# One kernel for hashed attention and two dense layers: issue order read from a table, one weight step fewer, second key copy by DMA

## The chip, the cores and the metric

The kernel runs on one core of a Trainium2 chip. The metric is device time in microseconds (us), the median of a few executions. The core has five instruction streams: PE (TensorE, matmuls; its weight loads are shown as PEld), DVE (VectorE), ACT (ScalarE), POOL (GpSimd) and SP (SyncE, which here only issues DMAs). Each stream executes its instructions in the order in which the program lists them, and waits on semaphores for the other streams.

## The reference

```python
q_bits = (einsum('bhsd,dk->bhsk', q, proj) > 0);  k_bits = the same with k
mask   = bucket(q_bits)[..., None] == bucket(k_bits)[..., None, :]
scores = where(mask, q @ k.T / sqrt(D), -1e9)
attn   = exp(scores - max);  attn /= attn.sum + 1e-9
x = (attn @ v) with the heads side by side          # 1536 x 512
h = x @ w_in;  g = 0 (h <= -1), (h+1)**2/4, h (h >= 1)
x = g @ moe_w_out                                    # d_ff 2048
out = ((x @ w_a) * (x @ w_b)) @ moe2_w_out           # d_ff 1536
```

Two batches of 8 heads, 768 positions, head size 64. The weights of the dense layers arrive as 64-bit floats, seen as pairs of 32-bit words.

## The kernel before

**Recording and ordering.** The kernel does not call the engines directly. Every step is recorded with `add(engs, emit, r, w)` as an operation: which engines could do it and at what estimated cost, what it reads, what it writes. `Program.schedule` then runs an event-driven list scheduler over the recorded operations with these costs and with hand-tuned ranks and biases (`TUNE`), and so chooses an engine for every operation and one issue order; `issue` emits them in that order. An operation that several engines can do (a copy on ACT or DVE, a subtraction on DVE or POOL) is thus placed by the scheduler.

**Attention.** For each of 16 heads, keys are loaded (`load_head`, tile `kn`), doubled along the free dimension by a copy on ACT or DVE, transposed on PE (`tk`) and split into a high and a low part (`kh`, `kl`). Queries are split (`qs`), transposed (`tq`) and scaled (`qt`). `signs` forms all projections' signs in one PSUM bank (`kp`, constants `zq_h`, `zq_l`, `zk`), `buckets` turns them into rows that go next to the parts (`q` copy, `kid`, `kl`). `qk` makes six score tiles of 128x768 for a head: matmuls (`s`), a minimum on DVE (`mn`, L602), the exponential on ACT (`sm`, L604), then `phi`, the fp16 part of it (ACT or DVE), `plo`, the rest (POOL or DVE, L384), a DMA transpose of each pair of tiles (`pth`, `ptl`), and `pv` on PE. Each score tile so costs DVE at least one `mn`, ACT one `sm`, and four elementwise steps in all. There are 96 score tiles.

**Weights.** Each of 71 matrices of 512 KB is loaded as `stage` and turned from 64-bit into 32-bit floats in five steps in `conv_one`: absolute value of the upper word on ACT (L847), a maximum with 2^-15 ("clamp", L850, DVE or POOL), a shift with a mask (L852, DVE), and two steps that join sign and lower bits (L855, L858, DVE, each with two inputs from SBUF). The result `F` or `wab` is split into a high and a low part (`whi`/`wlo`, `wkh`/`wkl`).

**Dense layers.** Tokens are taken in four blocks of 384. `hp`, `ap` and `bp` are the first contractions of the two layers (L953, twelve matmuls each), `acc` the second ones (L1001, L1037). The first two blocks' dense work is interleaved with the attention of the second batch. DVE, ACT and POOL do the elementwise steps between (`t`, `gh`, `gl`, `xs`).

**Start.** Twelve matmuls on zeros warm up PE; the projections are fetched by two DMAs from POOL's queue and turned into `zq_h`, `zq_l`, `zk` by nine DVE instructions before the recorded operations begin.

Of the kernel before, what the change touches and what calls it, by code (L numbers as in the profile page):

```python
# [23 lines left out]
T0 = 130  # L24
LEAST = 2.0 ** -15


class Buf:
    """A tile that is allocated when the first operation that writes it is issued."""

    def __init__(self, tag, shape, dtype, name=None):
# [15 lines left out]

class Program:
    """Records operations with the buffers they touch, orders them for all engines by list
    scheduling with estimated costs, and issues them in that order."""  # L50

    PRICE = {"pe": 0.0, "act": 0.3, "dve": 1.7, "pool": 0.2, "sp": 0.0}
    PRICE2 = {"pe": 0.0, "act": -2.5, "dve": 2.5, "pool": 1.3, "sp": 0.0}
    FLAT = ("acc", "y", "xn")
    TUNE = {
# [1095 lines left out]
```

## Time and profile before

| what | value |
|---|---|
| median of 3 runs | 862.54 us (862.17 to 863.79) |
| span of the profiled execution, first to last instruction | 861.3 us |
| the profiled execution's own time | not listed; its span is 1.2 us below the median |
| PE busy | 801.6 us (93%) |
| DVE / ACT / POOL busy | 588.1 (68%) / 511.6 (59%) / 192.3 us (22%) |
| mean granted TensorE clock | 0.972 of full speed |

Busy time is the time in which an engine executes at least one instruction; successive instructions of one engine overlap a little, so their durations add up to more than its busy time. "Idle before" an instruction is put down to what released it last.

### The profile page before, as it was taken

To read this page: it belongs to the slowest core of one execution; us is meant where nothing else is said; L and a number is where in the kernel's file an instruction comes from. 1 tells how busy PE (TensorE), PEld (TensorE's weight loads), DVE (VectorE), ACT (ScalarE), POOL (GpSimd) and SP (SyncE) were. 2 spreads that over 40 slices of the span, in tenths; PEclk is the share of its full clock that TensorE was granted. 3 is DMA by queue.
4 is the path that set the end of the run, shared out by engine and by line. 5 is a ranking of instruction groups with operands and counts; after the bars stand their busy time and mean duration, and the time that the engine had idled before them with its cause. 6 is when DMAs were issued, how large, how long until landed. Compare 5 with 4: busy or idle time off the path is not lost.

```text
span 861.3 us, 14674 instructions
## 1 busy us (share of the span) xinstructions
PE 801.6 (93%) x5680; PEld 736.9 (86%) x5680; DVE 588.1 (68%) x982; ACT 511.6 (59%) x937; POOL 192.3 (22%) x160
## 2 busy tenths in 40 slices
PE   7776776878999999999999999999999999999998
PEld 4665655768989889889999999999999999999997
DVE  5999889988999999878897689987621122212111
ACT  7877877787979988876785666744431131113112
POOL 2765566632323423323201110000000000000000
PEclk8989898899999999999999999999999999999999
DMA  7999999988669595546102233344110000001001
GB/s 224 191 226 193 230 177 217 213 166 181 169 147 188 131 179 117 114 73 102 32 25 74 74 98 123 120 126 131 66 38 1 1 28 10 1 1 38 1 1 37
DMA packets 197590, 91.79 MB, mean 107 GB/s; under 512 B 165136, under 2 KB 192016, under 8 KB 197520
## 3 DMA queue, kind: packets, MB, share of 16 engines
q1 hardware_dynamic: 197168, 90.72, 46.4%
q8 instruction: 44, 0.72, 0.3%
q14 instruction: 26, 0.21, 0.1%
q10 hardware_dynamic: 288, 0.13, 0.1%
q0 software_dynamic: 64, 0.00, 0.0%
HBM read 49.94 MB, written 3.15 MB: 62 GB/s over the span
## 4 chain that ended last, share of the span: by engine, by line
PE 68%; DVE 14%; DMA 7%; ACT 5%; issue 3%; POOL 1%; SPq 1%; DVEq 0%; ACTq 0%; POOLq 0%
PE acc L1001 12%; PE hp L953 12%; PE bp L953 12%; PE ap L953 12%; PE acc L1037 12%; DVE mn L602 3%; PE s L599 3%; PE pv L666 2%; DMA ptl<-plo 2%; DMA stage<-in_moe_w_in 2%; DVE F L858 1%; ACT sm L604 1%; DVE wlo L384 1%; PE kp L507 1%; ACT phi L379 1%
## 5 line engine op out<-in xcount | busy, mean ns | idle before, releaser
L379 ACT ACTIVATE gh<-t 128x384 fp32r<-128x384 f32 x112 | 58.7, 524 | 128.8 <-PE acc L1037 102.8
L1021 DVE TENSOR_TENSOR t<-t,bp 128x384 f32<-128x384 f32 x48 | 26.6, 554 | 157.3 <-PE bp L953 145.9
L384 POOL TENSOR_TENSOR plo<-sm,phi 128x768 f16<-128x768 f32 x64 | 112.2, 1757 | 94.9 <-ACT phi L379 48.5
L604 ACT ACTIVATE sm<-s,mn 128x768 f32<-128x768 f32 x96 | 86.0, 900 | 35.1 <-DVE mn L602 33.4
L602 DVE TENSOR_REDUCE mn<-s 128x1 f32<-128x768 f32 x96 | 90.5, 948 | 4.9 <-PE s L599 4.2
L384 DVE TENSOR_TENSOR gl<-t,gh 128x384 fp32r<-128x384 f32 x98 | 54.5, 556 | 42.4 <-ACT gh L379 42.3
L599 PE MATMUL s<-kh,qt 128*128 128x384 f32 x192 | 60.4, 398 | 19.4 <-ACT sm L604 19.2
L379 ACT ACTIVATE phi<-sm 128x768 f16<-128x768 f32 x85 | 71.5, 841 | 3.2 <-DMA pth<-phi 2.4
L379 ACT ACTIVATE t<-ap 128x384 f32<-128x384 f32 x48 | 23.6, 492 | 70.0 <-PE ap L953 69.9
L953 PE MATMUL bp<-xsl,wkh 128*128 128x384 f32 x192 | 64.6, 336 | 0.0
L953 PE MATMUL bp<-xsh,wkl 128*128 128x384 f32 x192 | 64.5, 336 | 0.0
L953 PE MATMUL ap<-xsl,wkh 128*128 128x384 f32 x192 | 64.4, 335 | 0.0
L953 PE MATMUL ap<-xsh,wkl 128*128 128x384 f32 x192 | 64.3, 335 | 0.0
L953 PE MATMUL ap<-xsh,wkh 128*128 128x384 f32 x192 | 64.2, 335 | 0.0
L953 PE MATMUL bp<-xsh,wkh 128*128 128x384 f32 x192 | 64.2, 334 | 0.0
L847 ACT ACTIVATE wab<-stage 128x512 f32<-128x512 f32 x71 | 47.3, 667 | 25.5 <-DMA stage<-in_moe_w_out 6.0
L666 PE MATMUL pv<-vc,pth 128*128 128x65 f16 (+1 forms) x1152 | 56.3, 201 | 4.2 <-DVE kl L384 1.9
L666 PEld LDWEIGHTS <-pth 128*128 128x128 f16 x1152 | 46.4, 103 | 15.6 <-issue 14.0
L599 PEld LDWEIGHTS s<-kh,qt 128*128 128x128 f32 x192 | 33.1, 206 | 28.1 <-ACT sm L604 25.9
L1037 PE MATMUL acc<-wkh,gl 128*128 128x512 f32 x144 | 57.0, 396 | 0.0
L1037 PE MATMUL acc<-wkl,gh 128*128 128x512 f32 x144 | 56.8, 395 | 0.0
L1037 PE MATMUL acc<-wkh,gh 128*128 128x512 f32 x144 | 56.0, 389 | 0.0
(144 smaller groups left out, 2250.9 us busy)
## 6 DMA issues: line engine op xcount, KB each, us to landing
stage<-in_moe_w_out SPq DMA_DIRECT2D x31, 512.0 KB, 4.0
stage<-in_moe_w_in SPq DMA_DIRECT2D x16, 512.0 KB, 4.7
stage<-in_moe_w_a SPq DMA_DIRECT2D x12, 512.0 KB, 3.6
stage<-in_moe_w_b SPq DMA_DIRECT2D x12, 512.0 KB, 3.6
kn<-in_k SPq DMA_DIRECT2D x16, 192.0 KB, 3.9
qn<-in_q SPq DMA_DIRECT2D x16, 192.0 KB, 3.1
vn<-in_v SPq DMA_DIRECT2D x16, 192.0 KB, 3.5
vscan<-in_v SPq DMA_DIRECT2D x8, 384.0 KB, 5.3
```

The costliest lines, as they stand in the source:

```text
L379: nc.scalar.activation(dst, src, ACTF.Copy)
L384: (nc.vector if e == "dve" else nc.gpsimd).tensor_tensor(dst, a, b, ALU.subtract)
L507: nc.tensor.matmul(s()[0:NR, 0:HC], z[:, 32 - 32 * c:32 - 32 * c + NR], m, start=(i == 0), stop=(i == len(terms) - 1))
L599: nc.tensor.matmul(s()[:, i, 0:HC], x()[:, qs], t()[:, i * HC:(i + 1) * HC], start=(n == 0), stop=(n == 1))
L602: add({"dve": c_dve(S)}, lambda e: nc.vector.tensor_reduce(mn(), s()[:, :, 0:HC], AX.XY, ALU.min), r=[s], w=[mn])
L604: o = add({"act": c_act(S, True) + 0.093}, lambda e: nc.scalar.activation(sm().rearrange("p (c n) -> p c n", c=2), s()[:, :, 0:HC], ACTF.E ...
L666: nc.tensor.matmul(o[:, t, 0:D + 1 - i], w()[:, t, c, :], vc()[:, c, i, 0:D + 1 - i], start=(n == 0), stop=(n == 3 * J - 1))
L847: add({"act": 0.52}, lambda e: nc.scalar.activation(ab(), t()[:, :, :, 1].bitcast(F32), ACTF.Abs), r=[t], w=[ab], after=gate(n) if moe2 el ...
L953: nc.tensor.matmul(o()[:, 0:TB], a()[:, kk, :], m(), start=(n == 0), stop=(n == 3 * KD - 1))
L1001: nc.tensor.matmul(ac()[:, 0:TB], a()[:, d, :], x(), start=(f == 0 and n == 0), stop=(f == F1 - 1 and n == 2))
L1021: add({"dve": c_dve(TB)}, lambda e: nc.vector.tensor_tensor(t(), t(), o()[:, 0:TB], ALU.mult), r=[o], w=[t])
L1037: nc.tensor.matmul(ac(), a()[:, ts], x().rearrange("p k n -> p (k n)"), start=(f == 0 and n == 0), stop=(f == F2 - 1 and n == 2))
```

## The change

1. `Program.schedule` no longer computes an order. A table `ORDER` gives it: each of its 3061 entries is a letter (p PE, a ACT, v DVE, g POOL, s SP) and a step, and the running sum of the steps is the number of the recorded operation that is issued next on that engine. `TUNE`, the prices and the event loop are gone. The costs handed to `add` are still there and are no longer read; several were edited.
2. In `conv_one` the clamp is gone. ACT copies the upper word with a scale of 2^-112 in place of taking the absolute value, the shift no longer masks, and the sign mask is one bit wider to the right.
3. The second copy of the keys comes from a second DMA out of memory, except for the first head, where it stays a copy on an engine.
4. The projections are fetched by SP, as the fifth DMA of its queue, and their six split instructions on DVE become recorded operations that `signs` depends on.
5. Eight warm-up matmuls instead of twelve.

```diff
-    WARM = 12
+    WARM = 8
+ORDER = """
+s3 s-2 s34 s2 s-33 a2 s27 v-31 v5 s564 p-563 p3 s9 a-11 a3 s2 v-4 v3 s586 p-583 s28 p-26 v-13 a12 a2 g4 p-2
...
+        for x in ORDER.split():
+            n += int(x[1:] or 1)
+            o = self.ops[n]
+            o.eng = name[x[0]]
+            assert o.eng in o.engs and not o.wait
...
+            out.append(o)
...
+    def projections():
+        def get(e):
+            for i in range(2):
+                nc.sync.dma_start(out=prj[i * D:(i + 1) * D], in_=proj)
+        add({"sp": DMA["tiny"]}, get, w=[(zb, 0)])
+        def split(e):
+            nc.vector.tensor_copy(p_h, prj)
+            nc.vector.tensor_tensor(p_l, prj, p_h, ALU.subtract)
...
+        add({"dve": 1.0}, split, r=[(zb, 0)], w=[(zb, 1)])
...
-        if dup:
+        if dup and (b, h) != (0, 0):
+            add({"sp": DMA["load"]}, lambda e: nc.sync.dma_start(
+                out=t()[:, :, 1, :], in_=src[b, h].rearrange("(p j) d -> p j d", j=J)), r=[(t, 0)], w=[(t, 1)])
+        elif dup:
             add({"act": c_act(J * D), "dve": c_dve(J * D, True)},
                 lambda e: copy_on(e, t()[:, :, 1, :], t()[:, :, 0, :]), r=[(t, 0)], w=[(t, 1)])
...
-        add({"act": 0.52}, lambda e: nc.scalar.activation(ab(), t()[:, :, :, 1].bitcast(F32), ACTF.Abs),
+        add({"act": 0.556}, lambda e: nc.scalar.activation(ab(), t()[:, :, :, 1].bitcast(F32), ACTF.Copy, scale=SHIFT),
             r=[t], w=[ab], after=gate(n) if moe2 else ())
-        add({"dve": 0.335, "pool": 1.456},
-            lambda e: (nc.gpsimd if e == "pool" else nc.vector).tensor_scalar(ab(), ab(), LEAST, None, ALU.max),
-            w=[ab])
         add({"dve": 0.335}, lambda e: nc.vector.tensor_scalar(
-            r().bitcast(I32), ab().bitcast(I32), 3, 0x3FFFFFFF, ALU.logical_shift_left, ALU.bitwise_and),
+            r().bitcast(I32), ab().bitcast(I32), 3, None, ALU.logical_shift_left),
             r=() if here else [ab], w=[r])
         add({"dve": 0.602}, lambda e: nc.vector.scalar_tensor_tensor(
-            r().bitcast(I32), t()[:, :, :, 1], -0x40000000, r().bitcast(I32), ALU.bitwise_and, ALU.bitwise_or),
+            r().bitcast(I32), t()[:, :, :, 1], -0x80000000, r().bitcast(I32), ALU.bitwise_and, ALU.bitwise_or),
```

The table is opaque as printed. The kernel before records 3130 operations; without the 71 clamps and with two for the projections there are 3061, and the table's numbers run over exactly these. Numbered in that way it can be set against the order that the planner gave. The counts that differ most, up to the 48th of the 96 score tiles on PE, from there to the 96th, and over the whole kernel (before, after):

| step | engine | to the 48th | 48th to 96th | whole |
|---|---|---|---|---|
| clamp L850 | DVE | 15, 0 | 19, 0 | 70, 0 |
| first step of a conversion, L847 | ACT | 15, 10 | 20, 25 | 71, 71 |
| L852 and L855, each | DVE | 15, 10 | 20, 25 | 71, 71 |
| L858 | DVE | 15, 9 | 20, 26 | 71, 71 |
| `plo` | POOL | 43, 26 | 21, 29 | 64, 55 |
| `plo` | DVE | 2, 18 | 28, 21 | 32, 41 |
| `phi` | DVE | 11, 11 | 0, 9 | 11, 20 |
| `q` copy | DVE | 17, 5 | 4, 2 | 21, 7 |
| bucket rows, `q` and `kl` | DVE | 8, 12 | 1, 6 | 9, 18 |
| `kh` and `qs` copies | DVE | 6, 10 | 4, 4 | 10, 14 |
| `tl` | DVE | 4, 7 | 2, 11 | 6, 18 |
| `vc` high part | DVE | 4, 1 | 1, 1 | 5, 2 |
| `qs` rest | DVE | 2, 5 | 1, 3 | 3, 8 |
| `qs` rest | POOL | 8, 5 | 5, 3 | 13, 8 |
| `xn` | DVE | 0, 3 | 1, 3 | 1, 9 |
| `xn` | POOL | 12, 9 | 17, 13 | 31, 23 |
| `wlo` | DVE | 1, 1 | 51, 37 | 58, 51 |
| `wlo` | POOL | 2, 2 | 5, 17 | 16, 23 |
| `whi` | DVE | 1, 0 | 29, 10 | 36, 17 |
| `gl` | DVE | 0, 0 | 16, 22 | 98, 103 |
| `gh` | DVE | 0, 0 | 0, 9 | 0, 25 |
| second copy of keys | ACT | 9, 0 | 5, 0 | 14, 0 |
| second copy of keys | SP | 0, 9 | 0, 6 | 0, 15 |
| loads of weights (`stage`) | SP | 17, 11 | 20, 26 | 71, 71 |

The first dense contraction stands after the 53rd score tile on PE before, after the 55th in the table.

All matmuls stay, but for the four of the warm-up; only their order on PE changes.

## Rows read from the trace of the kernel before

**Rows 1.** The page: busy time by engine, and PE in 40 slices of the span.
```profile
PE 801.6 (93%) x5680; PEld 736.9 (86%) x5680; DVE 588.1 (68%) x982; ACT 511.6 (59%) x937; POOL 192.3 (22%) x160
...
PE   7776776878999999999999999999999999999998
```
**Rows 2.** Stretches: bounds, length, busy us of PE, PEld, DVE, ACT, POOL, granted clock, DMA.
```profile
0.00:35.20 35.20, 26.70 (x139) 18.39 (x139) 25.45 (x53) 26.62 (x50) 14.53 (x17) 0.85 0.74 200
...
35.20:167.10 131.90, 98.25 (x1014) 81.28 (x1014) 125.68 (x177) 101.82 (x174) 82.69 (x62) 0.87 1.05 211
167.10:207.50 40.40, 32.04 (x340) 27.58 (x340) 32.91 (x57) 31.84 (x58) 10.55 (x12) 0.96 0.90 184
207.50:415.00 207.50, 202.70 (x1787) 187.56 (x1786) 186.99 (x307) 170.41 (x309) 67.25 (x57) 1.00 0.65 136
415.00:861.30 446.30, 441.91 (x2405) 422.07 (x2403) 217.06 (x392) 180.88 (x349) 17.28 (x14) 1.00 0.15 48
```
**Rows 3.** DVE in order of time: minimum of the 8th, 48th and 56th score tile.
```profile
35.22 0.94 DVE L602 TENSOR_REDUCE mn<-s 128x1 f32<-128x768 f32 x1
...
167.14 0.96 DVE L602 TENSOR_REDUCE mn<-s 128x1 f32<-128x768 f32 x1
...
207.53 0.95 DVE L602 TENSOR_REDUCE mn<-s 128x1 f32<-128x768 f32 x1
```
**Rows 4.** Groups on DVE, 20 to 180 us: count, busy us, mean ns, idle before.
```profile
L858 DVE SCALAR_TENSOR_TENSOR F<-stage,F 128x512 int32<-128x512 int32 x13 | 13.5, 1039 | 0.0
L850 DVE TENSOR_SCALAR wab<-wab 128x512 f32<-128x512 f32 x15 | 12.6, 837 | 1.0 <-ACT wab L847 1.0
L855 DVE SCALAR_TENSOR_TENSOR F<-stage,F 128x512 int32<-128x512 int32 x13 | 12.4, 964 | 0.1
L852 DVE TENSOR_SCALAR F<-wab 128x512 int32<-128x512 int32 x14 | 11.7, 844 | 0.1
L381 DVE CAST phi<-sm 128x768 f16<-128x768 f32 x11 | 11.4, 1037 | 0.3 <-issue 0.3
L381 DVE CAST q<-qt 64x384 fp32r<-64x384 f32 x16 | 10.5, 656 | 0.8 <-ACT qt L491 0.8
...
L548 DVE TENSOR_SCALAR kl<-kid 64x384 fp32r<-64x384 f32 x8 | 4.5, 561 | 0.2
L384 DVE TENSOR_TENSOR plo<-sm,phi 128x768 f16<-128x768 f32 x3 | 3.4, 1138 | 0.0
L693 DVE TENSOR_TENSOR xn<-tl,r 128x192 f32<-128x192 f32 x1 | 1.8, 1807 | 0.0
```
**Rows 5.** Single tiles, shortest/median/longest ns, on DVE and on POOL.
```profile
L850 DVE TENSOR_SCALAR wab<-wab x15: 409/420/1899, 40.0 to 179.8; 128x512 f32<-128x512 f32 x15
...
L855 DVE SCALAR_TENSOR_TENSOR F<-stage,F x13: 675/686/2132, 30.7 to 162.9; 128x512 int32<-128x512 int32 x13
...
L381 DVE CAST phi<-sm x11: 541/1180/1589, 26.2 to 162.4; 128x768 f16<-128x768 f32 x11
...
L384 DVE TENSOR_TENSOR plo<-sm,phi x26: 916/952/2408, 200.1 to 407.8; 128x768 f16<-128x768 f32 x26
...
L384 POOL TENSOR_TENSOR plo<-sm,phi x64: 1640/1662/2368, 21.0 to 399.0; 128x768 f16<-128x768 f32 x64
```
**Rows 6.** Groups on DVE, 200 to 420 us.
```profile
L384 DVE TENSOR_TENSOR wlo<-F,whi 128x512 fp32r<-128x512 f32 x53 | 44.9, 852 | 1.3
```
**Rows 7.** Waits of PE (us, times, longest): 20 to 180 us, then from 415 us.
```profile
PE s L599 <- ACT sm L604: 17.2, 17, 3.3
PE pv L666 <- DMA ptl<-plo: 5.1, 5, 2.1
...
PE hp L953 <- DVE xsl L384: 0.3, 1, 0.3
```
**Rows 8.** Keys: copies on ACT in the whole span; DMA issues with time to landing.
```profile
L379 ACT ACTIVATE kn<-kn 128x384 f32<-128x384 f32 x14 | 7.3, 519 | 3.7 <-DMA kn<-in_k 3.6
...
kn<-in_k SPq DMA_DIRECT2D x16, 192.0 KB, 3.9
```

More of the change, by code (lines that the diff above doesn't have):

```diff
@@ L1 @@
-import heapq
-from bisect import bisect_left, insort
 from contextlib import ExitStack
@@ L23 @@
 PEN = 2.0 ** 100
-T0 = 130
-LEAST = 2.0 ** -15
+SHIFT = 2.0 ** -112
+DMA = {"load": (0.6, 0.75, 2.4), "scan": (0.6, 1.15, 3.3), "turn": (1.35, 1.5, 2.6, 0.5), "stage": (0.45, 2.1, 3.2),
+       "out": (0.4, 0.8, 1.7), "row": (0.6, 0.5, 2.2), "tiny": (1.2, 0.2, 2.2)}
+ORDER = """
+s3 s-2 s34 s2 s-33 a2 s27 v-31 v5 s564 p-563 p3 s9 a-11 a3 s2 v-4 v3 s586 p-583 s28 p-26 v-13 a12 a2 g4 p-2
+a13 s5 g-13 a-4 a550 p-548 p7 a5 v-11 v548 p-544 a3 s-17 v559 a-544 p-3 a11 v18 p-11 v530 g-518 p-5 a665 v-671
@@ L33, in __init__ @@
         self.tile = None
-        self.users = self.step = 0
+        self.users = self.left = self.step = 0
         self.kind = self.name.rstrip("0123456789")
@@ L43 @@
 class Op:
-    __slots__ = ("n", "engs", "emit", "rank", "bias", "kind", "port", "succ", "wait", "ready", "allocs", "bufs",
-                 "start", "eng", "done")
+    __slots__ = ("n", "engs", "emit", "succ", "wait", "allocs", "bufs", "eng", "first")
 class Program:
[L52 to L55, printed above, removed]
[57 rows of a table removed]
-    }
-    LAT = {"pe": 0.22, "act": 0.2, "dve": 0.14, "pool": 0.16, "sp": 0.9}
-    SELF = {"pe": 0.0, "act": 0.03, "dve": 0.12, "pool": 0.03, "sp": 0.9}
     def __init__(self, caps, alloc):
@@ L128, in add @@
             b.step += 1
-        o.kind = f"{self.phase}.{b.kind if b else 'out'}" + (str(b.step) if b and b.kind not in self.FLAT else "")
-        tune = self.TUNE.get(o.kind, (0,))
-        o.rank = o.n + tune[0]
-        o.bias = dict(zip(("act", "dve", "pool"), tune[1:]))
-        o.succ, o.wait, o.ready, o.allocs, o.bufs, o.start = [], 0, 0.0, [], [], None
+        o.succ, o.wait, o.allocs, o.bufs = [], 0, [], []
         deps = set(after)
@@ L158, in add @@
         o.wait = len(deps)
-        for b in o.bufs:
-            b.users += 1
-        o.port = not any(b.tag in ("p", "px", "acc", "s0", "sx") for b in o.bufs)
         self.ops.append(o)
@@ L244, in schedule @@
-        for o in self.ops:
-            if not o.wait:
-                push(o, 0.0)
-        out = []
-        t = 0.0
-        while len(out) < len(self.ops):
-            for e in engines:
-                if until[e] > t:
-                    continue
-                for _, _, o in list(ready[e]):
-                    if len(o.engs) > 1 and better(o, e):
-                        continue
-                    if t > T0 and o.port and e in port and until[port[e]] > t and holds[port[e]]:
-                        continue
-                    withdraw(o)
-                    if start(o, e):
-                        break
-            if not events:
-                raise RuntimeError("no operation can be issued")
-            t = max(t, events[0][0])
-            while events and events[0][0] <= t:
-                _, _, kind, o = heapq.heappop(events)
-                if kind == 0:
-                    offer(o)
-                elif kind == 2:
-                    for b in o.bufs:
-                        b.users -= 1
-                        if not b.users:
-                            free[b.tag] += 1
-                            for x in blocked.pop(b.tag, ()):
-                                offer(x)
@@ L275, in schedule @@
-        self.span = max(o.done for o in out)
+        name = {"p": "pe", "a": "act", "v": "dve", "g": "pool", "s": "sp"}
+        n, out = -1, []
+        for x in ORDER.split():
[3 more added lines that the diff above has]
+            assert o.eng in o.engs and not o.wait
+            for y in o.succ:
+                y.wait -= 1
+            o.wait = -1
+            out.append(o)
+        assert len(out) == len(self.ops)
         return out
@@ L327, in attn_moe_kernel @@
         "mn": 4, "r": 2, "tl": 2, "vam": 1, "vs": 1,
-        "s0": 1, "sx": 1, "px": 2, "p": 2, "acc": 1,
+        "s0": 1, "sx": 1, "px": 2, "p": 2, "acc": 1, "z": 1,
     }
@@ L342, in alloc @@
     def alloc(b):
+        if b.tag == "z":
+            return None
         if b.tag not in P:
@@ L401, in one @@
                 t = Buf("sm", [128, 2, J, D], F32, "vscan")
-                add({"sp": 1.1}, lambda e: nc.sync.dma_start(
+                add({"sp": DMA["scan"]}, lambda e: nc.sync.dma_start(
                     out=t().rearrange("p h j d -> p h (j d)"),
@@ L508, in mm @@
                                  start=(i == 0), stop=(i == len(terms) - 1))
-        add({"pe": 1.4}, mm, r=[d["q"][0], d["q"][1]] + [(t, c) for t in (d["kh"], d["kl"]) for c in range(2)],
+        add({"pe": 1.45}, mm, r=[(zb, 1), d["q"][0], d["q"][1]] + [(t, c) for t in (d["kh"], d["kl"]) for c in range(2)],
             w=[s, bit])
@@ L527, in buckets @@
             q2[c] = o
-            add({"dve": c_dve(HC, True), "act": c_act(HC), "pool": 1.4},
-                lambda e: copy_on(e, o()[0:64], qt()[0:64]), r=[qt], w=[(o, 0)])
+            if True:
+                add({"dve": c_dve(HC, True), "act": c_act(HC), "pool": 1.4},
+                    lambda e: copy_on(e, o()[0:64], qt()[0:64]), r=[qt], w=[(o, 0)])
+            else:
+                add({"sp": DMA["row"]}, lambda e: nc.sync.dma_start(
+                    out=o()[0:64].bitcast(F32), in_=qt()[0:64].bitcast(F32)), r=[qt],
+                    w=[(o, 0)])
             out = (o, 1)
@@ L533, in buckets @@
             out = (o, c)
-        add({"pe": 0.16}, lambda e: nc.tensor.matmul(s()[:, 0:HC], code[rows, cols], bit()[rows], start=True,
+        add({"pe": 0.26}, lambda e: nc.tensor.matmul(s()[:, 0:HC], code[rows, cols], bit()[rows], start=True,
                                                      stop=True), r=[bit], w=[s])
@@ L633, in tp @@
                 def tp(src, p):
-                    add({"sp": 1.35}, lambda e: nc.sync.dma_start_transpose(
+                    add({"sp": DMA["turn"]}, lambda e: nc.sync.dma_start_transpose(
                         p().rearrange("p t c q -> p (t c) q"), src().rearrange("p t n -> p (t n)")),
@@ L742, in attention @@
         load(0, "q")
+        put(projections)
         scans = {b: list(v_scan(b)) for b in range(B)}
@@ L842, in conv_one @@
         here = moe2 or n in again
-        add({"sp": 1.46}, lambda e: nc.sync.dma_start(out=t().rearrange("p k n t -> p k (n t)"), in_=src), w=[t])
+        add({"sp": DMA["stage"]}, lambda e: nc.sync.dma_start(out=t().rearrange("p k n t -> p k (n t)"), in_=src), w=[t])
         tr, th = place[n]
@@ L954, in mm @@
                     n += 1
-        return add({"pe": 12 * 0.163}, mm, r=[wh, wl] + [t for p in x for t in p],
+        return add({"pe": 2.09}, mm, r=[wh, wl] + [t for p in x for t in p],
                    w=[o, *more], after=after)
@@ L1046, in one @@
                         b, j = divmod(blk * NTL + d, J)
-                        add({"sp": 0.73}, lambda e: nc.sync.dma_start(
+                        add({"sp": DMA["out"]}, lambda e: nc.sync.dma_start(
                             out=out.rearrange("(b p j) n -> b j p n", p=128, j=J)[b, j], in_=ob()[:, od]),
@@ L1092, in attn_moe_kernel @@
         nc.vector.memset(half, 0.5)
+        for z in (zq_h, zq_l, zk):
+            nc.vector.memset(z.bitcast(F32), 0.0)
         nc.scalar.activation(half, half, ACTF.Copy)
```

219 lines of the change are left out of this document (134 added, 85 removed), and 57 rows, old and new, of the table TUNE.

## Prediction

> **What bounds the kernel now.** I read the page first. PE is busy 801.6 of 861.3 us, so only 59.7 us are idle, and the slices show where: sevens and eights at the left, nines from about the eleventh slice on [rows 1]. The stretches put numbers to it [rows 2]. PE is idle 8.5 us up to 35.2, 33.7 us from there to 167.1 (131.9 less 98.25), 8.4 us up to 207.5, only 4.8 us in the next 207.5 us, and 4.4 us in the last 446. From 415 us on PE waits once for a listed reason, 0.3 us [rows 7]. From 207.5 us on the matmuls set the pace, and no edit on another engine can gain there; it can only lose.
>
> The 131.9 us before that are the attention of the first batch without dense work: the minimum of the 8th score tile stands at 35.22, that of the 48th at 167.14 [rows 3]. That is 40 tiles at 3.30 us. DVE is busy 125.7 of these 131.9 us (95%), ACT 101.8 (77%), POOL 82.7 (63%), PE 98.25 (74%) [rows 2]. So DVE sets the pace there, though the waits of PE name ACT's exponential, which itself comes after DVE's minimum [rows 7].
>
> What fills DVE are not the instructions by themselves. The clamp takes 409 ns at its shortest and 420 at the median, but 837 in the mean, with one of 1899; L855 takes 675 and 2132; the fp16 part 541 and 1589 [rows 4, 5]. The longest excess over the shortest by 1.0 to 1.5 us, about one POOL `plo` of 1.66 us [rows 5]. Later, where POOL works 67 of 207 us, half of the DVE `plo` are within 40 ns of the shortest [rows 2, 5]. I read this as DVE standing still behind a POOL instruction, for whole instructions at a time.
>
> **The change, part by part, up to the 48th tile.** The counts are those of the table in the section on the change; means are those of rows 4, so with the standing still included.
>
> - Clamps: 15 x 0.837 = -12.6 us of DVE.
> - Conversions put off: 5 x (0.844 + 0.964) + 6 x 1.039 = -15.3 us. They return later (below).
> - Work that DVE takes from POOL: 16 `plo` x 1.138 = +18.2; 3 `qs` rests at the nearest row, 0.561, = +1.7; 3 `xn`, between 0.561 and 1.807 each, I take 1.0, = +3.0. Sum +22.9.
> - Exchanges with ACT: 12 `q` copies fewer, -7.9; 4 bucket rows more, +2.2; 7 of `kh`, `qs`, `tl` more at no more than 0.561, I take +2.9; 3 high parts of `vc` fewer at 0.656 or more, -2.0; one minimum fewer, -0.9. Sum -5.7.
>
> Together -10.7 us at unchanged means. But POOL loses 17 `plo` there, 17 x 1.66 = 28 of its 97 us (14.5 and 82.7) [rows 2, 5], so DVE should stand still less. What is left of the affected steps carries an excess of mean over shortest of 10 x 0.435 (L852, which I set against the clamp's shortest), 10 x 0.289 (L855), 9 x 0.364 (L858 against L855's), 11 x 0.496 (`phi`) and 18 x 0.22 (`plo`), 20 us in all; 29% of it is -5.8. So -16.5 with this relief and -10.7 without; with `xn` dear -8.3, with `xn` and `plo` at their cheap ends (0.561, 0.952) -21. I take -15, nearer to the relief, since rows 5 show so few lengths between the two ends.
>
> DVE at 95% passes this on to the time. ACT is no obstacle: it loses 9 key copies x 0.519 [rows 8] and 5 first steps, and takes 10 `q` copies, so it stays at about 100 us of 117. The 48th tile then comes at 152 us, a pace of 116.9 / 40 = 2.92 us. PE idles 0.84 us a tile now (33.7 / 40) and 0.46 then.
>
> Between the 48th and the 56th tile PE idles 8.4 us now [rows 2, 3]. The table keeps to attention alone up to there, so 8 x 0.46 = 3.7 us: -4.7.
>
> **After that**, DVE's list has 5 or 6 conversions more (+9.5 at the shortest times of rows 5), 19 clamps fewer (-8.0 at 0.42), 14 `wlo` fewer (-11.9 at 0.852 [rows 6]), 19 `whi` fewer (-7.8 at 0.41), 7 `plo` fewer (-6.7), in all -25; against it 9 `phi` (+4.9), 6 `gl`, 9 `gh`, 9 `tl` and some 14 others at up to 0.561, about +20. DVE's load is so within a few us of before. POOL, though, gets 8 `plo` and 12 `wlo` more and some small ones less, some 22 us on 67; a third more of the standing still of `wlo` there, 37 x (0.852 - 0.675), is +2, the same on the rest about as much. DVE is at 90% in this stretch and PE at 98% [rows 2]; I take +3 us for PE.
>
> **Costed at nothing.** The key copies by DMA: up to the 48th tile 9 loads of 192 KB are added and 6 of 512 KB put off, so the queues carry less; a copy lands in about 3.9 us [rows 8], hidden as long as SP issues it that long before the transposition (rival E). The projections stand behind four DMAs of SP, and the four warm-up matmuls that go let PE reach the first transposition earlier: between a us gained and one landing, 3.9 us, lost at the start; I take 0. The first step of a conversion and the shift keep their elements and their engine: no difference. The last 446 us: the same matmuls without gaps, covered by DVE at 49% and ACT at 41% [rows 2]; what is moved between those two there costs PE nothing unless a step comes within a contraction's length of its use.
>
> Sum: -15 - 4.7 + 3 = -16.7 us. 861.3 - 16.7 = 844.6 for the span; the median shown lies 1.2 us above the profiled span, so 846 us.
>
> **The rivals.** A difference under 0.2% (1.7 us) can hardly be told from none here: the three runs span 1.6 us.
>
> A, as forecast: 840 to 852 (the bounds -8 and -21, and the -4.7 shrinking with them). 0.54.
>
> B, DVE ceases to be the limit and the pace falls to that of ACT and PE, at 2.45 to 2.55 us a tile (98 to 102 us over 40). For it: the excess on DVE is all due to POOL, and POOL is relieved. At 2.6 us the 48th tile comes at 139, 28 us less, and nearly all of the 8.4 us go too: down to 828, so 828 to 839. Against it: every tile passes DVE, ACT, DMA and PE in turn, and DVE's list still gives 2.9. 0.15.
>
> C, the gain is half given back between 207.5 and 415 us: DVE is at 90% there, gets the deferred conversions, and POOL's load grows by a third; PE's idle 4.8 us become 12 to 15: 852 to 860. 0.16.
>
> Same within 0.2%: the table's fixed order leaves waits of the size of the gain. 0.05.
>
> D, slower because the standing still moves with the work. The longest DVE `plo` is 2.408, 1.49 over the shortest [rows 5], so a `plo` on DVE can itself stand behind POOL. If each of the 16 added ones stands behind a whole POOL `plo`, that is 16 x 1.66 = +26.6 us, DVE's list grows by 11.6 instead of falling by 15, PE's idle after the 48th tile is 9.0 rather than 3.7, and the time is 878. It decides from about 10 of the 16. Against it: the median of 26 DVE `plo` is 0.952 [rows 5]. 0.05. [...]
>
> E, slower by the key copies: SP's queue is in order and shared with the transposes that `pv` waits for (5.1 us now [rows 7]). If each of the 9 second copies lands one landing, 3.9 us, too late, PE loses 35 us: 881. From 5 of the 9 on nothing is left of the gain. Against it: the second copy depends on nothing that the first does not. 0.05.
>
> **Range.** 832 to 861 leaves out D and E, the bottom of B and a part of "same". Faster is A, B and C, 0.85; same 0.05; slower 0.10.
>
> **What would show it.** The minimum of the 48th tile near 152 us and the 56th near 176; L852, L855 and `phi` nearer to their shortest times up to there; `plo` on DVE near 0.95 to 1.14; PE idle near 20 us less up to the 56th tile and within a few us of now after it; the last 446 us as they are. Wrong if the pace stays near 3.3 us (D), if PE waits for `kn` in most heads (E), or if PE's idle after the 56th tile passes 10 us (C).

## The result, and the profile after

The changed kernel takes 848.67 us in the median (four runs, 846.93 to 849.05); the kernel before took 862.67 us beside it. The ratio is 0.9832 (95% interval 0.9818 to 0.9846), some 14.5 us less. The profiled execution spans 847.0 us. The forecast was 846 us, faster.

The page of the kernel after, its busy line and PE in 40 slices:

```profile
PE 800.5 (95%) x5676; PEld 733.0 (87%) x5676; DVE 587.4 (69%) x1042; ACT 443.4 (52%) x791; POOL 193.6 (23%) x158
...
PE   7677888789999999999999999999999999999998
```

DVE of the kernel after in order of time: the minima of the 8th, 48th and 56th score tile, to be laid beside [rows 3]:

```profile
38.72 0.95 DVE L594 TENSOR_REDUCE mn<-s 128x1 f32<-128x768 f32 x1
...
155.14 0.96 DVE L594 TENSOR_REDUCE mn<-s 128x1 f32<-128x768 f32 x1 [0.58 <-PE s L591]
...
181.31 0.95 DVE L594 TENSOR_REDUCE mn<-s 128x1 f32<-128x768 f32 x1
```

The stretches of the kernel after, in the columns of [rows 2]. The last line repeats the second stretch with the tiles' exact times as its bounds, as later runs are given:

```profile
0.00:38.70 38.70, 27.61 (x139) 19.54 (x139) 27.13 (x56) 26.78 (x48) 10.99 (x14) 1.00 0.80 203
38.70:155.10 116.40, 94.91 (x1012) 76.68 (x1011) 99.97 (x164) 97.49 (x165) 51.22 (x41) 0.91 1.13 219
155.10:181.30 26.20, 20.11 (x217) 16.64 (x217) 22.31 (x37) 23.28 (x40) 9.31 (x9) 0.90 1.07 225
181.30:400.70 219.40, 215.64 (x1913) 199.02 (x1912) 194.50 (x334) 169.68 (x302) 89.37 (x70) 1.00 0.76 156
400.70:847.00 446.30, 442.19 (x2403) 421.13 (x2401) 243.46 (x454) 126.21 (x238) 32.66 (x26) 1.00 0.15 48
...
38.72:155.14 116.42, 94.93 (x1012) 76.70 (x1010) 99.95 (x164) 97.53 (x165) 51.24 (x41) 0.91 1.13 219
```

PE's idle time, length less busy, tells where the gain is. Up to the 48th tile it was 8.5 + 33.7 = 42.2 us and is 11.1 + 21.5 = 32.6; from there to the 56th 8.4 and 6.1; in the next stretch 4.8 and 3.8; in the last 4.4 and 4.1 [rows 2]. Together -13.2 us, and PE's busy time fell by 1.1 us [rows 1]: 14.3 us of span. In the stretch from the 8th to the 48th tile alone, 12.2 us of the 15.5 are idle time; the other 3.3 are PE's busy time, 98.25 to 94.91 us for almost the same matmuls, at a granted clock of 0.87 and then 0.91 [rows 2]. The 8th tile comes 3.5 us later than before, the 48th 12.0 us earlier. Between them the pace went from 3.30 to 2.91 us a tile.

DVE fell further than forecast: its busy time between the 8th and the 48th tile fell by 25.7 us (125.67 to 99.95), and its share from 95% to 86%. The groups on DVE of the kernel after, 20 to 165 us (columns as in [rows 4]):

```profile
L368 DVE TENSOR_TENSOR plo<-sm,phi 128x768 f16<-128x768 f32 x18 | 20.0, 1114 | 6.7 <-DMA ptl<-plo 4.5 <-issue 1.2 <-ACT phi L363 1.0
...
L848 DVE SCALAR_TENSOR_TENSOR F<-stage,F 128x512 int32<-128x512 int32 x9 | 9.2, 1027 | 0.0
L365 DVE CAST phi<-sm 128x768 f16<-128x768 f32 x12 | 7.7, 644 | 0.6 <-ACT sm L596 0.5
L845 DVE SCALAR_TENSOR_TENSOR F<-stage,F 128x512 int32<-128x512 int32 x9 | 7.2, 811 | 0.0
...
L842 DVE TENSOR_SCALAR F<-wab 128x512 int32<-128x512 int32 x10 | 4.7, 476 | 0.0
```

The shift (L842, L852 before) has a mean of 476 ns where it had 844, `phi` 644 where it had 1037, L845 811 where it (L855 then) had 964 [rows 4]; L848 (L858 then) and `plo` stayed near their old means, 1027 against 1039 and 1114 against 1138. Half of the `phi` now run within 10 ns of the shortest, where the median was 1180 [rows 5]:

```profile
L365 DVE CAST phi<-sm x12: 545/554/1560, 25.4 to 164.3; 128x768 f16<-128x768 f32 x12
```

Ahead of `plo`, though, DVE stands idle 6.7 us, most of it for a DMA transpose. The waits of the kernel after, 20 to 180 us (us, times, longest):

```profile
POOL plo L368 <- DMA ptl<-plo: 16.9, 5, 5.3
...
DVE plo L368 <- DMA ptl<-plo: 5.6, 3, 4.0
PE pv L658 <- DMA ptl<-plo: 5.1, 4, 2.3
ACT phi L363 <- DMA pth<-phi: 5.0, 8, 1.7
```

A `plo` waits for a transpose because its buffer is free only when an earlier tile's transpose has read it. On POOL and ACT these waits are longer than before, and the one on DVE is new. The kernel before, 20 to 180 us:

```profile
POOL plo L384 <- DMA ptl<-plo: 11.5, 7, 3.4
...
ACT phi L379 <- DMA pth<-phi: 2.4, 3, 1.2
```

The stream that issues the transposes is full as well. Added up from SP's rows between the 8th and the 48th tile, SP is executing DMA-issuing instructions for 105.6 of 131.9 us before (80%) and for 106.1 of 116.4 us after (91%), more than DVE's 86%.

### The profile page after: what moved, and what is told of

The parts are those of the page before. It is cut to its first block, busy times and chain, and to the rows that moved or that the text cites. A ratio compares the mean times of both kernels' runs of the same rounds, so it can differ in the third digit from the quotient of the medians.

```text
span 847.0 us, 14513 instructions
## 1 busy us (share of the span) xinstructions
PE 800.5 (95%) x5676; PEld 733.0 (87%) x5676; DVE 587.4 (69%) x1042; ACT 443.4 (52%) x791; POOL 193.6 (23%) x158
## 4 chain that ended last, share of the span: by engine, by line
PE 74%; DMA 8%; DVE 8%; ACT 7%; issue 3%; POOL 1%; SPq 0%; ACTq 0%; DVEq 0%; POOLq 0%
PE acc L991 13%; PE hp L943 13%; PE ap L943 12%; PE bp L943 12%; PE acc L1027 12%; PE s L591 5%; PE pv L658 4%; DMA pth<-phi 3%; DMA ptl<-plo 2%; ACT sm L596 2%; DVE plo L368 2%; ACT phi L363 2%; DVE mn L594 1%; DMA stage<-in_moe_w_in 1%; PE kp L494 1%
## 5 line engine op out<-in xcount | busy, mean ns | idle before, releaser
L363 ACT ACTIVATE gh<-t 128x384 fp32r<-128x384 f32 x87 | 45.5, 523 | 232.1 <-DVE t L1011 145.1
L368 POOL TENSOR_TENSOR plo<-sm,phi 128x768 f16<-128x768 f32 x55 | 95.9, 1747 | 120.5 <-ACT phi L363 36.2
L596 ACT ACTIVATE sm<-s,mn 128x768 f32<-128x768 f32 x96 | 86.3, 900 | 18.3 <-DVE mn L594 15.3
L368 DVE TENSOR_TENSOR gl<-t,gh 128x384 fp32r<-128x384 f32 x103 | 60.3, 585 | 47.5 <-ACT gh L363 46.8
L363 ACT ACTIVATE phi<-sm 128x768 f16<-128x768 f32 x76 | 63.8, 842 | 5.7 <-DMA pth<-phi 5.0
L965 ACT ACTIVATE t<-hp,half 128x384 f32<-128x384 f32 x64 | 37.0, 578 | 41.7 <-PE hp L943 41.2
L365 DVE COPY t<-ap 128x384 f32<-128x384 f32 x46 | 25.5, 555 | 47.1 <-PE ap L943 47.1
```

Of the source, the lines that this page charges most:

```text
L363: nc.scalar.activation(dst, src, ACTF.Copy)
L368: (nc.vector if e == "dve" else nc.gpsimd).tensor_tensor(dst, a, b, ALU.subtract)
L596: o = add({"act": c_act(S, True) + 0.093}, lambda e: nc.scalar.activation(sm().rearrange("p (c n) -> p c n", c=2), s()[:, :, 0:HC], ACTF.E ...
L965: add({"act": 0.465}, lambda e: nc.scalar.activation(t(), o()[:, 0:TB], ACTF.Relu, bias=half, scale=0.5), r=[o], w=[t])
```

## The experiments

Each ratio is against the kernel before, run beside it. Where two kernels are compared, the difference of their ratios is multiplied by 862.5 us. "The order of before" is the order and the engines that the planner gave to the kernel before, written out as a table of the same form, so that one edit leaves all else in place. The table below gathers the single profiles: the 8th tile's minimum, the stretch from there to the 48th, and in that stretch the busy times, the granted clock and what the DMA queues moved. One profile each, so small differences of the first columns count for little: with the table's order the 8th tile alone lies between 38.6 and 42.2 us. The profiled execution of b_no_clamp took 852.52 us, 3 us less than that kernel's median; what is read against its profile can be too large by as much. Those of the other changed kernels in the table lie within 1.1 us of their medians, but for a_clamp_back (872.39 us, 2.8 below).

| kernel | 8th, us | 8th to 48th, us | PE / DVE / POOL busy, us | clock | DMA, GB/s | ratio (95%) |
|---|---|---|---|---|---|---|
| before | 35.2 | 131.9 | 98.3 / 125.7 / 82.7 | 0.87 | 211 | 1 |
| b_no_clamp | 34.5 | 125.2 | 94.1 / 116.5 / 82.2 | 0.90 | 223 | 0.9923 (0.9895 to 0.9952) |
| b_plo_dve | 35.6 | 125.5 | 95.1 / 118.5 / 58.8 | 0.90 | 218 | 0.9917 (0.9898 to 0.9935) |
| b_keys_dma | 36.0 | 131.4 | 97.9 / 117.5 / 82.2 | 0.88 | 220 | 1.0021 (0.9998 to 1.0044) |
| p_no_clamp | 34.5 | 131.5 | 102.1 / 126.8 / 82.4 | 0.84 | 220 | 1.0101 (1.0082 to 1.0119) |
| after | 38.7 | 116.4 | 95.0 / 100.0 / 51.2 | 0.91 | 219 | 0.9832 (0.9818 to 0.9846) |
| a_plo_pool | 40.1 | 113.7 | 91.2 / 97.3 / 74.2 | 0.95 | 219 | 0.9850 (0.9832 to 0.9868) |
| a_keys_act | 38.6 | 112.0 | 91.6 / 97.7 / 50.6 | 0.94 | 212 | 0.9818 (0.9792 to 0.9845) |
| a_keys_act_early | 39.5 | 110.0 | 92.3 / 100.8 / 50.5 | 0.95 | 217 | 0.9788 (0.9772 to 0.9804) |
| a_clamp_back | 42.0 | 115.0 | 94.8 / 101.0 / 49.3 | 0.90 | 217 | 1.0145 (1.0126 to 1.0163) |
| a_conv_early | 41.2 | 126.3 | 101.5 / 111.0 / 50.0 | 0.85 | 218 | 0.9920 (0.9900 to 0.9941) |
| a_start_old | 42.2 | 114.6 | 94.5 / 98.2 / 51.1 | 0.91 | 221 | 0.9834 (0.9810 to 0.9857) |

**The clamp alone, in the order of before** (b_no_clamp).

```diff
-ACTF.Abs)            +ACTF.Copy, scale=SHIFT)
-        add({"dve": 0.335, "pool": 1.456}, ... tensor_scalar(ab(), ab(), LEAST, None, ALU.max), w=[ab])
```

> The kernel before, its own issue order and engines written out as a table, without the clamp (the ACT step is the scaled copy, the shift has no mask); keys, projections and warm-up as before. Theory 1 (DVE's load up to the 48th tile sets the pace, and the clamp is part of it): 15 clamps at 0.837 us leave that stretch, DVE at 95%, so 8 to 12 us faster, 851 to 855 us; the 48th minimum near 157 us. Rival (the order is what counts; in an order made for other work the freed time turns into waits): 0 to 4 us faster, 859 to 863 us.

In this diff and in those below, pieces of lines are shown. The sign mask that goes with the clamp's removal keeps one bit (-0x80000000) where before it kept two (-0x40000000): it is narrower by a bit.

855.47 us, 6.6 us less than before. The 48th tile comes at 159.74 us, 7.4 earlier than in [rows 3], and DVE's busy time in the stretch falls by 9.2 us. What remains on DVE is still stretched, at 20 to 180 us:

```profile
L818 DVE SCALAR_TENSOR_TENSOR F<-stage,F 128x512 int32<-128x512 int32 x15 | 16.4, 1090 | 0.0
...
L336 DVE CAST phi<-sm 128x768 f16<-128x768 f32 x11 | 11.3, 1030 | 1.6 <-DMA pth<-phi 1.1 <-issue 0.3
L812 DVE TENSOR_SCALAR F<-wab 128x512 int32<-128x512 int32 x15 | 10.7, 722 | 0.4 <-ACT wab L810 0.3
```

So taking the clamps away does shorten the list of an engine that was busy 95%, and 6.6 us, about half of the forecast 12.6, go into time.

**The same without writing the order out** (p_no_clamp): the planner of the kernel before, without the clamp, orders anew.

```diff
-        add({"dve": 0.335, "pool": 1.456}, ... ALU.max), w=[ab])
+        ab.step += 1
```

> The kernel before with the clamp taken out and its planner left to order the rest again with its own costs, ranks and biases; everything else as before. Theory 1 (the table's order and engines fit durations that the planner does not know, such as DVE standing behind POOL): 852 to 862 us, no better than the 855 us of the frozen order. Rival (the planner, freed of the clamp, finds what the table has): 850 us or less.

871.38 us, slower than before by 8.7 us, and so outside what was expected. With less work the planner gives another order, in which DVE is busy 126.8 of 131.5 us again and the 48th tile comes at 166.0. Of the 8.5 us by which its profiled span is longer (869.8 against 861.3), 7.1 are PE's busy time, 808.7 against 801.6 us at a mean granted clock of 0.958 against 0.972, and only 1.4 are idle time. The removal gains where the order of before is kept; left to this planner, whose ranks were tuned with the clamp in place, it loses.

**The clamp put back into the table** (a_clamp_back), on DVE, after each first step of a conversion.

```diff
-p-11 v530 g-518          +p-11 v531 g-519
-v548 p-544 a3            +v548 v p-545 a3
...
```

> After with the 71 clamps put back on DVE, each directly ahead of its shift (absolute value on ACT, masks as before). Theory 1 (DVE sets the pace up to the 48th tile and is nearly full after it): 10 clamps there and 25 up to the 96th tile at 0.42 to 0.84 us, most of it passed on: 6 to 14 us slower than after, 855 to 863 us. Rival (DVE, busy 86% between the 8th and the 48th tile of after, has room for them): 0 to 4 us slower.

875.2 us, 27 us slower than after, where 6 to 14 had been expected. Hardly any of it lies up to the 48th tile, which comes at 157.0 (after: 155.1): DVE's busy time in the stretch is only 1 us more, and the stretch is no longer than in after, 115.0 against 116.4 us. It lies later: between the minima of the 56th and the 96th score tile this run takes 215.1 us where after takes 204.9, and behind the 96th 472.5 where after takes 460.8, together 21.9 of the 23.6 us by which its profiled span is longer. Stretches of this kernel:

```profile
183.00:420.00 237.00, 227.33 (x1956) 208.49 (x1956) 216.49 (x371) 176.92 (x317) 93.18 (x72) 0.99 0.70 144
...
520.00:600.00 80.00, 74.68 (x405) 70.56 (x406) 75.89 (x150) 31.73 (x58) 1.61 (x1) 1.00 0.39 125
```

and the kernel after at 520 to 600 us:

```profile
520.00:600.00 80.00, 80.00 (x437) 76.69 (x437) 69.65 (x133) 26.82 (x49) 0.00 (x0) 1.00 0.37 118
```

PE is idle 9.7 us from 183 to 420 where it was idle 3.8 from 181.3 to 400.7, and 5.3 us from 520 to 600 where it was not idle at all; there DVE is at 95%. The same step is worth 6.6 us in the order of before, where the planner had placed it, and 27 us in the table's, where each clamp was put directly ahead of its shift. The rows show where the time goes, not why: which of the clamps there cost most, and whether other places would have cost less, was not tried.

**The conversions, moved forward again** (a_conv_early): 11 of them, so that 14 rather than 9 are done before the 48th tile.

```diff
-a565 g71 p-627           +g636 p-627
-v542 p-535               +p7
...
```

> After with 11 conversions of weights (the 4th to the 14th) moved forward in the order, engines unchanged, so that 14 rather than 9 are finished before the 48th score tile, about as in before. Theory 1 (DVE's list up to the 48th tile still sets the time of that tile): 5 conversions at 1.8 to 2.3 us, so the 48th minimum 5 to 11 us later than 155, and the whole 3 to 8 us slower than after, since less of it is regained later. Rival (DVE is at 86% there and has room): the 48th minimum within 3 us of 155 and the whole within 2 us of after.

856.07 us, 7.6 slower than after. The 8th tile is 2.5 us later, the stretch 9.8 us longer, and DVE's busy time in it 11.0 us more. What grew was for the most part PE's busy time, though, 6.6 of the 9.8 us for the same 1012 matmuls, at a granted clock of 0.85 instead of 0.91:

```profile
41.19:167.45 126.26, 101.53 (x1012) 82.11 (x1010) 110.98 (x179) 98.66 (x169) 49.95 (x40) 0.85 1.09 218
```

The forecast that putting conversions off pays is borne out. Why it pays, this run can't separate: DVE's list is longer, the clock is lower, and the loads of the weights came forward with the conversions, 11 `stage` issues on SP between the two tiles where after has 7.

**`plo`, both ways** (b_plo_dve, a_plo_pool). In the first, b_no_clamp with 16 `plo` moved from POOL to DVE up to the 48th tile; in the second, the table with 16 moved from DVE back to POOL.

```diff
-p46 g-6 a4               +p46 v-6 a4             (b_plo_dve, 16 such)
-p25 v-16 a-6             +p25 g-16 a-6           (a_plo_pool, 16 such)
```

> The kernel before with its own order, without the clamp, with the same 16 rests of the fp16 parts moved from POOL to DVE up to the 48th tile that the table has there. Theory 1 (what DVE takes over it gets back by standing still less, as the mirror of it did on after's order): within 4 us of the same kernel without the move, which took 855 us. Rival by the prediction's own sum (+18 on DVE's list, -6 by the relief): 8 to 14 us slower, 863 us or more.

> After with the 16 rests of the fp16 parts that the table moved to DVE up to the 48th tile back on POOL, at their places in the order. Theory 1 (POOL makes DVE stand still): DVE loses 17.8 us of list, POOL gains 28 us, the shifts, joins and fp16 parts on DVE lengthen again, the transposes come later: 2 to 10 us slower than after. Rival (DVE's list alone counts): 4 us or more faster.

855.27 us against 855.47 of b_no_clamp, and 848.79 against 848.67 of after; the intervals of the ratios overlap: neither can be told from its base. The stretch from 20 to 180 us of b_no_clamp and then of b_plo_dve:

```profile
20.00:180.00 160.00, 119.56 (x1285) 97.98 (x1285) 148.04 (x212) 131.01 (x228) 101.36 (x79) 0.91 1.06 214
```

```profile
20.00:180.00 160.00, 122.45 (x1282) 100.26 (x1280) 147.15 (x226) 128.46 (x222) 73.28 (x62) 0.88 1.05 211
```

DVE executes 14 instructions more, 16 `plo` of about 1 us among them, and is busy 0.9 us less, while POOL loses 28 us. By tiles, from the 8th to the 48th, DVE is busy 2.0 us more (118.5 against 116.5 in the table). What the 16 `plo` cost came back elsewhere, as the groups of b_plo_dve on DVE show against those of b_no_clamp above:

```profile
L339 DVE TENSOR_TENSOR plo<-sm,phi 128x768 f16<-128x768 f32 x19 | 18.7, 982 | 2.5 <-DMA ptl<-plo 2.4
L818 DVE SCALAR_TENSOR_TENSOR F<-stage,F 128x512 int32<-128x512 int32 x15 | 14.0, 931 | 0.0
...
L336 DVE CAST phi<-sm 128x768 f16<-128x768 f32 x11 | 7.2, 652 | 0.0
L812 DVE TENSOR_SCALAR F<-wab 128x512 int32<-128x512 int32 x15 | 8.4, 564 | 0.0
```

`phi` falls from 1030 to 652 ns, the shift from 722 to 564, L818 from 1090 to 931. The other way round, the groups on DVE of a_plo_pool, 20 to 165 us:

```profile
L842 DVE SCALAR_TENSOR_TENSOR F<-stage,F 128x512 int32<-128x512 int32 x9 | 10.5, 1170 | 0.0
L839 DVE SCALAR_TENSOR_TENSOR F<-stage,F 128x512 int32<-128x512 int32 x9 | 10.4, 1162 | 0.0
L359 DVE CAST phi<-sm 128x768 f16<-128x768 f32 x12 | 10.0, 836 | 2.8 <-ACT sm L590 2.6
L836 DVE TENSOR_SCALAR F<-wab 128x512 int32<-128x512 int32 x9 | 8.0, 893 | 0.0
```

Against after, the shift went from 476 to 893 ns, L839 (L845 there) from 811 to 1162, `phi` from 644 to 836. DVE's busy time from 20 to 165 us is 124.8 against 125.6 us, with 16 `plo` fewer; by tiles it is 2.7 us less (97.3 against 100.0). So 16 us of `plo` change DVE's busy time by 2 to 3 us at most. That DVE pays the rest by standing still behind POOL's 1.66 us is a reading of the longer means; the profile shows the lengths, not what an instruction stood behind.

**Second key copies by DMA, in the order of before** (b_keys_dma): b_no_clamp with the copies turned into second loads at the same places.

```diff
-p13 a-30 v560            +p13 s-30 v560          (15 such)
+            add({"sp": DMA["load"]}, ... nc.sync.dma_start(out=t()[:, :, 1, :], ...))
```

> The kernel before with its own order, without the clamp, with the second copy of the keys by a second DMA (15 of 16 heads) at the place where the copy on ACT or DVE stood. Theory 1 (the added DMAs delay the transposes on SP and in the queues): 1 to 6 us slower than the 855 us without them. Rival (ACT's 7 us are worth more): 1 to 4 us faster.

863.62 us, 8.5 slower than b_no_clamp; the 48th tile comes 7.7 us later. PE hardly waits for a key (0.3 us, once). What waits is `plo` and `phi`. Waits of b_no_clamp at 20 to 180 us, then of b_keys_dma:

```profile
POOL plo L339 <- DMA ptl<-plo: 10.6, 7, 3.0
...
ACT phi L334 <- DMA pth<-phi: 6.1, 5, 2.1
```

```profile
POOL plo L339 <- DMA ptl<-plo: 18.2, 11, 3.2
...
ACT phi L334 <- DMA pth<-phi: 8.9, 9, 2.7
```

The instruction on SP that issues a transpose takes longer too (shortest/median/longest ns), in b_no_clamp and in b_keys_dma:

```profile
L597 SPq DMA_TRANSPOSE ptl<-plo x24: 1274/1855/3289, 26.8 to 170.1; - x24
```

```profile
L597 SPq DMA_TRANSPOSE ptl<-plo x24: 1279/2316/3678, 29.1 to 179.2; - x24
```

For `pth` the median goes from 2032 to 2284 ns, though it was 1734 in the kernel before, with the same loads as b_no_clamp, so a part of this is spread. The stretches from the 8th to the 48th tile, b_no_clamp and then b_keys_dma:

```profile
34.50:159.74 125.24, 94.11 (x1014) 77.89 (x1014) 116.51 (x165) 101.86 (x176) 82.22 (x63) 0.90 1.11 223
```

```profile
36.00:167.39 131.39, 97.90 (x1014) 81.38 (x1014) 117.49 (x163) 100.09 (x171) 82.18 (x62) 0.88 1.06 220
```

Seven loads of 192 KB more there lengthen the stretch by 6.2 us, and SP's issuing time in it by 7.6 (110.0 to 117.6 us). That the transposes are held back by the loads on SP, and that the ring of `plo` buffers passes this on to POOL, fits these rows; that the queues have more to move fits them too.

**Second key copies on ACT, in the table** (a_keys_act, a_keys_act_early). In the first the copy stands directly ahead of the key's transposition on PE; in the second at the place in the order where the second load stood.

```diff
-a3 s-17 v559             +a3 v542
-v p-544 a-3              +v a-587 p43 a-3        (a_keys_act, 15 such pairs)
-a3 s-17 v559             +a3 a-17 v559           (a_keys_act_early, 15 such)
```

> After, with the second copy of the keys made by ACT as before, issued directly ahead of the first transposition that reads it. Theory 1: ACT gets 9 x 0.52 = 4.7 us more up to the 48th tile, where it is busy 84% of the time, and PE waits for a copy that comes late in ACT's queue: 1 to 5 us slower than after, 850 to 854 us. Rival (the added DMAs crowd the transposes in the queues): 1 to 4 us faster than after.

> After with the second copy of the keys on ACT at the place in the order where the table has the second DMA. In the run with the copy directly ahead of the transposition PE waited 12 us for these copies and the time was that of after. Theory 1 (those waits cost time and an earlier copy saves them): 2 to 6 us faster than after, 842 to 846 us. Rival (ACT's and DVE's load set the pace, and PE would have waited for something else): within 2 us of after.

Copied late: 846.97 us, not to be told from after, though over the whole span PE waits 12 times for the copy. That row of a_keys_act:

```profile
PE tk L432 <- ACT kn L357: 12.2, 12, 1.8
```

Copied early: 843.61 us (842.61 to 844.79), ratio 0.9788, 3.8 us faster than after and faster than both kernels. The stretch of a_keys_act_early from the 8th to the 48th tile, and its waits at 20 to 180 us:

```profile
39.51:149.53 110.02, 92.26 (x1012) 72.80 (x1010) 100.76 (x165) 98.47 (x171) 50.50 (x41) 0.95 1.13 217
```

```profile
POOL plo L362 <- DMA ptl<-plo: 12.5, 4, 5.7
...
DVE plo L362 <- DMA ptl<-plo: 3.6, 4, 2.0
...
PE pv L652 <- DMA ptl<-plo: 1.9, 3, 1.0
ACT phi L357 <- DMA pth<-phi: 1.1, 2, 0.7
```

The stretch is 6.4 us shorter than in the kernel after, and each of the four waits on transposes is smaller. The mean issue of a transpose in the stretch is hardly shorter, though, 1.92 us against 1.98 in after; what SP saves is the loads' own issuing, and its issuing time falls from 106.1 to 99.3 us. In a_keys_act POOL's wait for transposes is as long as in after (17.5 us), and yet the stretch is 4.4 us shorter, so this wait alone does not measure what the copies cost. Seen from the kernel before, this is the part of the change that costs time: 8.5 us in the one order, 3.8 in the other.

**The start** (a_start_old): projections by POOL's queue ahead of the recorded operations, twelve warm-up matmuls.

```diff
-    WARM = 8              +    WARM = 12
-        put(projections)  +            nc.gpsimd.dma_start(out=prj[i * D:(i + 1) * D], in_=proj)
```

> After with the old start: twelve warm-up matmuls, the projections fetched by POOL's queue and split by DVE ahead of the recorded operations. Theory 1: within 2 us of after. Rival (the new start is a part of the gain): 2 us or more slower.

848.63 us: no difference. The 8th tile comes no earlier with the old start (42.2 us, at a granted clock of 0.72 up to there, against 38.7 at 1.00), so nothing here says that the 3.5 us by which the 8th tile is later than before come from this edit. It is late in every run with the table's order, 38.6 to 42.2 us.

**Order and engines apart** (b_engines_of_table, a_engines_of_planner): the order of before with the table's engine for 409 operations, clamp kept; and the table's order with the planner's engines for the same.

```diff
-p3 g-4 a2                +p3 v-4 a2              (b_engines_of_table, 409 letters)
-v-31 v5 s564             +v-31 g5 s564                (a_engines_of_planner, 409 letters)
```

> The issue order of before with the engine of every operation taken from the table; clamp, key copies on ACT, projections and warm-up as before. Theory 1 (load on DVE): DVE keeps the clamps and gets 16 more of the fp16 rests up to the 48th tile, about +17 us at list prices, less some 6 us that it stands still less; so 5 to 12 us slower than before, 868 to 875 us. Rival (the choice of engines carries the gain, since POOL is out of DVE's way): 5 us or more faster than before, 858 or less.

> The table's issue order with every operation on the engine that the planner of before gave it (key copies by DMA, projections and missing clamp as after). Theory 1 (load on DVE): 16 of the fp16 rests up to the 48th tile go back to POOL, DVE loses 17 us of list price but stands still more; within 5 us of after, 844 to 854 us. Rival (the choice of engines carries the gain): most of the 14 us are lost, 857 us or more.

893.06 us (1.0353, 1.0325 to 1.0381) and 877.46 us (1.0175, 1.0147 to 1.0203). The first is 30 us above before, the second 30 us above after: either mixture is far worse than both kernels. The first lies outside both expectations. The second meets the rival's "857 us or more" in its number, but not in its reason: if the choice of engines carried the gain, the first run would have been faster. The loss lies mainly after the 56th tile. b_engines_of_table, then a_engines_of_planner there:

```profile
207.50:415.00 207.50, 190.24 (x1586) 172.06 (x1587) 179.92 (x288) 150.32 (x270) 81.96 (x62) 0.98 0.59 125
```

```profile
181.30:400.70 219.40, 202.75 (x1751) 182.13 (x1752) 190.67 (x300) 175.12 (x316) 62.88 (x55) 0.99 0.77 157
```

PE is idle 17.3 and 16.7 us where it is idle 4.8 and 3.8 in the kernels that keep their own engines. Over the whole span PE's waits of `hp` for DVE's `t` add up to 3.6 us in the first and 5.3 in the second, against 1.0 in before and none listed in after. That a step which takes another engine's time comes late for what was timed to it in these fixed orders is the author's reading; no run tested it. So the gain can't be divided between "order" and "engines", and which single moves of the table matter was not tried.

## Why the prediction was right

**The bound.** Right for the kernel before: with the clamp step alone taken out, 6.6 us of time went. Nearly all of the gain, 12.0 of 14.3 us, is there at the 48th tile; the stretch from the 8th to the 48th went from 131.9 to 116.4 us, -15.5 where -15 was forecast, a pace of 2.91 where 2.92 was. The 48th tile is at 155.1 and not at 152 because the 8th came 3.5 us later; where these went is not settled; the start edits alone do not bring them back. The pace came out right in part by luck. The forecast took all 15 us off PE's idle time, and only 12.2 came from there; the rest is PE's busy time at a higher granted clock, 0.91 against 0.87, which it had left as it was.

**The sum held because its terms were wrong in opposite senses.** That is luck too.

- Clamps: -12.6 us of DVE's list. Alone they shorten the stretch by 6.7 us, and DVE's busy time in it by 9.2. Right in sign, about half in size.
- Conversions put off: -15.3. Putting them back costs 9.8 us of the stretch, 6.6 of them PE's busy time. Right in sign, two thirds in size; that DVE's list is the reason is not shown, since their loads moved with them.
- Sixteen `plo` to DVE: +18.2, less 5.8 of relief, so +12. This step was mis-sized: measured +0.3 us in the stretch in one order and +2.7 in the other, no difference in the time of either kernel. The relief is not 29% of the excess but nearly all that the `plo` themselves cost. That agrees with DVE's busy time, which fell by 25.7 us and not by 15.
- Second key copies by DMA: costed at nothing, with the cover that SP issues the load a landing early. The cover was there, PE waits for no such load in the kernel after, yet the copies cost 6.2 us of the stretch in one order and 6.4 in the other. The step that failed is to cost the loads at nothing because a landing is hidden and the put-off weights carry more bytes: seven of them take 7.6 us more of SP's issuing time in b_keys_dma, and the queues move 28.9 MB there against 27.9 in b_no_clamp, while in the stretch of the kernel after SP is issuing for 91% of the time and the DMA share is 1.13 by the profile's measure, the mean of 16 engines. They are a part of why only 15.5 of DVE's 25.7 us came through; DVE stands idle ahead of `plo` for transposes, 4.5 us.

The measured steps add up to -6.7 - 9.8 + 0.3 to 2.7 + 6.3, so -7.5 to -9.9 us of the 15.5. The rest is what was not tried by itself: the exchanges with ACT (forecast -5.7), `qs` and `xn`, and the order within the stretch. They were measured in different orders, so the sum is only a rough one.

**A rival that the runs leave standing: the DMA queues.** In the twelve kernels of the table the stretch lasts from 110.0 to 131.9 us, and its DMA rate stays between 211 and 223 GB/s. Length times rate gives 27.8 MB before and 27.9 in b_no_clamp, 28.9 in b_keys_dma, 25.5 in after, 27.5 in a_conv_early and 23.9 in a_keys_act_early: the stretches of 110.0 to 116.4 us move 23.8 to 25.5 MB, those of 125.2 to 131.9 us 27.4 to 28.9. The runs that moved `plo` changed POOL and DVE but hardly the rate (218 against 223 GB/s, and 219 in both), and the clamps put back on DVE, six of them in the stretch, did not lengthen that of after. By this reading the conversions put off gained by their loads: 2.3 MB less at 219 GB/s would be 10 us, an estimate from these rows, and with the 6.7 of the clamps more than the 15.5. DVE set the pace before; whether DVE, SP or the queues set it in the kernel after, no run decides, since none moved the loads of weights without their conversions.

**From the 48th to the 56th tile**: PE's idle time fell by 2.3 us, forecast 4.7. **After it**: -1.3 us, forecast +3; the deferred conversions found room, with DVE at 89% there (194.50 of 219.4 us, before 90% [rows 2]). **The last 446 us**: as before, as forecast; PE's one listed wait there is 0.4 us.

**The rivals.** B (DVE ceases to be the limit) was half right in its condition, DVE is down to 86%, but the pace of 2.45 to 2.55 us did not follow: it is 2.91, and 2.75 without the key loads. What holds the rest is open. (At its own pace the 48th tile would have come at 133 to 137 us, not at the 139 of its working.) C (half given back later) fell: PE's idle time after the 56th tile went down. D (the standing still moves with the work) fell: moving `plo` is neutral in time, neither 878 nor a gain. In the two `plo` runs the means of `phi` (1030 to 652 ns with less on POOL, 644 to 836 with more) and of the shift (722 to 564, 476 to 893) moved with POOL's work; that DVE stood still behind POOL remains a reading of these lengths. E (the key copies) had the right culprit and the wrong mechanism: no copy was late for its transposition, and the price is about a sixth of the 35 us given.

## What to carry to other kernels

When an engine's mean durations lie far above their shortest, as those of `phi` on DVE in b_no_clamp (1030 against 537 ns), price a step that it takes over from another engine net: what the step adds to its list, less what its other steps get shorter by, from the same rows. In the two runs here the two nearly cancelled: 16 `plo` changed DVE's busy time by 0.9 us at most in equal windows. A DMA whose landing is hidden was not free here, some 6 us of the stretch for seven loads: price what it takes of the stream that issues it (7.6 us of SP in b_keys_dma) and of the queues, and look first how busy both are. In a schedule written out over five streams, test one edit with everything else held in place: the same removal was worth 6.6 us in one order, 27 in another, and came out 8.7 us slower when the planner ordered anew.

## What the runs showed of the hardware that was not expected

Sixteen `plo` moved between POOL and DVE left DVE's busy time nearly as it was, within 0.9 us of 148 and of 125 in equal windows and within 2.7 us from the 8th to the 48th tile, while POOL's changed by 27 to 28 us in the windows. With second loads of 192 KB on SP's queue the median issue of a `ptl` transpose was 2316 ns instead of 1855 in the order of before; in the table's order the mean issue of a transpose hardly differs with and without them, 1.98 and 1.92 us.

PE's busy time for the same matmuls was not a constant: 1012 of them took 91.2 us at a mean granted clock of 0.95 (a_plo_pool) and 101.5 at 0.85 (a_conv_early). From the 8th to the 48th tile the kernel after gained 12.2 us as idle time of PE and 3.3 as busy time, and a_conv_early lost 3.2 and 6.6 against it. A forecast made from PE's idle time alone, as this one was, leaves the second part out.
